# A spectral filter at its own row pitch, one Newton chain on VectorE, and 14 output buffers for the last generator

## The chip, the cores and the metric

The kernel runs on one core of a Trainium2 chip. A core has TensorE (PE: matmuls into PSUM, with the load of weights, PEld, beside them), VectorE (DVE), ScalarE (ACT), GpSimd (POOL) and SyncE (SP), which issues all the DMAs of this kernel. The metric is the device time of one launch in microseconds (us); lower is better. The time before the change is 369.65 us, the median of five runs between 368.98 and 370.34.

## The reference, cut to what matters

A block with two residual halves, its output and the gradients of all its inputs but one:

```python
def _A_ref(x, w_r, w_i):                       # spectral mixer
    X = rfft2(x, axes=(-2, -1))                # x: (1, 2048, 448)
    X = X * (w_r + 1j * w_i)                   # w: (2048, 225)
    return irfft2(X, s=(S, D), axes=(-2, -1))

def _B_ref(x, w1, b1, w2, b2):                 # token MLP, F = 1792
    h = _layernorm(x)
    u = gelu(einsum("bsd,sf->bdf", h, w1) + b1)
    return transpose(einsum("bdf,fs->bds", u, w2) + b2, (0, 2, 1))

h  = x + _A_ref(_layernorm(x), w_r, w_i)
h2 = h + _B_ref(_layernorm(h), w1, b1, w2, b2)
# outputs: h2 and vjp(grad_out) for x, w_r, w_i, w1, b1, w2, b2
```

Everything that goes in and comes out is bfloat16. The filter W has S = 2048 rows (one for each frequency along the sequence) of DF = 225 columns (half of 448, plus 1). Its gradient has the same shape and is output 2 (real part) and 3 (imaginary part).

## The kernel before, in words

The 2-D Fourier transforms are done as matmuls with cosine and sine tables that the kernel makes itself. A transform along D works on rows (`row_a`, `row_b`), one along the sequence is split in two steps, the second of which (`s2_stage`) works on 16 groups g of frequencies, 128 on the partitions, with (group, real or imaginary part, column) in the free dimension. Columns are padded there from 225 to KW = 226.

PE's order is written out by hand. Beside the chain of the transforms runs a list `pending` of generators that hold independent matmuls, and `fill(n)` takes n pieces from it wherever the transforms would leave PE without work. In the forward pass that list is `dg_gen` (the gradient at the GELU's output, 14 blocks of 16 matmuls, each with weights that come by a transposing DMA from w2, `load_w2T`); in the backward pass it is `gw_gen`, once for the gradient of w2 (output 6) and once for that of w1 (output 4).

The stages on PE in order of time are: rows of x with dG blocks (to about 50 us), the forward `s2_stage` with multiplication by W (50 to 86), the inverse rows (86 to 104), the MLP forward and its output (105 to 199), the MLP backward (199 to 246), the backward `s2_stage` (about 263 to 304), the inverse rows for the gradient of x with the second `gw_gen` (about 310 to 353), and the rest of that generator (to 361).

What the change and the prediction touch, by the lines of the kernel before:

- Row statistics and 1/sigma of the first layer norm. `ln_stats` runs on DVE. Rows 0 to 3 take a square root on ACT; rows 4 and 5 take a Newton chain on GpSimd (`newton_gp`, lines 367 to 376: 10 small operations on 128 x 2 values), called at line 844; rows 6 to 15 take the same chain two by two (line 879). `scale_R(t)` on DVE needs 1/sigma of row t; its result rX is the moving operand of `row_a(t)` on PE, whose stationary operand is made by `fold_prep` on DVE. `newton` (lines 353 to 365) is the same chain with 9 operations for DVE; before the change nothing calls it.
- The load of W. `w_load` (line 567) brings each plane (real, imaginary) of W into a helper region rB with four DMAs: partitions 0 to 63, 64 to 111, 112 to 127 and one row apart. Rows for partitions from 64 up have to be in reverse order of the groups, so they are loaded in forward order, one long run for a partition, and `w_place` (line 576) copies all of W from rB to its place `W_view_F` in rG, with the groups of the upper half reversed: 16 copies of 64 x 4 x 225, each given to ACT or DVE by `evac`, which weighs the two engines' loads (`Meter`). The copies are spread over the forward `s2_stage`, two by two from c2 = 3 on (line 672). The first four DMAs are issued in rows 9 to 12, the other four when the forward `s2_stage` begins, in SP's order T W W W W T T T, where T is a weight transpose for dG (line 897).
- The multiplication. `w_mult` (line 697) makes two products of a pair of groups with the real and the imaginary plane, broadcast over the two parts (128 x 904 elements), and two sums, all on DVE. In the backward pass `bwd_mult` (line 1189) does the same with the conjugate, and makes the gradient of W from two more products and two sums, written over W in place.
- W between the passes. It is stored to DRAM (`w_d`, line 915) and loaded again into rC (line 1250). Its gradient goes out from rC with `w_io` (line 551): eight DMAs, whose SBUF side is runs of 225 elements, spread over the rows of the last stage (`GW_AT`).
- Output buffers. Both `gw_gen` generators evict PSUM into the ring `ost`, six buffers of 1024 columns in rO (line 1200). An eviction into a buffer waits until the store from it, six buffers ago, has landed. rG holds `goT`, the moving operand of the first generator, which is done before the second one starts.

Of the kernel before, what the change touches and what calls it, by code (L numbers as in the profile page):

```python
# [98 lines left out]
class Ring:  # L99
# [20 lines left out]
def kernel(  # L120
# [58 lines left out]
    def evac(out, in_, scale=None):  # L179
        n = int(np.prod(in_.shape[1:]))  # L180
        if load[0] + sc.cost('copy', n, False) <= load[1] + ve.cost('tensor_copy', n, in_.dtype == BF16):
            if scale is None:
                sc.copy(out=out, in_=in_)
            else:
                sc.activation(out=out, in_=in_, func=ACT.Copy, scale=scale)
        elif scale is None:
            ve.tensor_copy(out=out, in_=in_)
        else:
            ve.tensor_scalar(out=out, in0=in_, scalar1=scale, scalar2=None, op0=ALU.mult)
# [89 lines left out]
    smc = mem.tile([P, 2, 16], BF16, name="smc")  # L279

    h_d = dram.tile([S, D], BF16, name="h_d")
    w_d = dram.tile([P, NG * 2 * KW], BF16, name="w_d")


    x_pt = A_x[0].rearrange("(p t) d -> p t d", t=NT)
# [259 lines left out]

    W_view_F = cut(rG, 0, NG, 2, KW)
    W_view_B = cut(rC, 0, NG, 2, KW)

    def w_io(Wv, dr, di, store):
        for c_, d in ((0, dr), (1, di)):
            for p0, p1, g0, g1, row, dims in ((0, 64, 0, 16, 0, [[16 * DF, 4], [1, 16 * DF]]),
                                              (64, 112, 0, 16, 112, [[-DF, 48], [1, DF]]),
                                              (112, 128, 1, 16, 127, [[-DF, 15], [1, DF]]),
                                              (112, 128, 0, 1, 64, [[1, DF]])):
                sb = Wv[p0:p1, g0:g1, c_, 0:DF]
                d_ap = bass.AP(d.tensor, d.offset + row * DF, [[P * DF, 16]] + dims)
                if store:
                    nc.sync.dma_start(out=d_ap, in_=sb)  # L560
                else:
                    nc.sync.dma_start(out=sb, in_=d_ap)
                yield

    W_rows = cut(rB, 0, 2, NG, DF)

    def w_load():
        for c_, d in ((0, A_w_r), (1, A_w_i)):
            for p0, p1, j0, j1, row, dims in ((0, 64, 0, 16, 0, [[16 * DF, 4]]), (64, 112, 0, 16, 97, [[-16 * DF, 3]]),
                                              (112, 128, 0, 15, 113, []), (112, 128, 15, 16, 64, [])):  # L570
                nc.sync.dma_start(out=W_rows[p0:p1, c_, j0:j1, :],
                                  in_=bass.AP(d.tensor, d.offset + row * DF,
                                              [[P * DF, 16]] + dims + [[1, (j1 - j0) * DF]]))
                yield

    def w_place():
        for g in range(0, NG, 4):
            for c_ in range(2):
                for p0, p1, src in ((0, 64, W_rows[0:64, c_, g:g + 4, :]),
                                    (64, P, W_rows[64:P, c_, NG - 1 - g:(NG - 5 - g if g < 12 else None):-1, :])):  # L580
                    evac(out=W_view_F[p0:p1, g:g + 4, c_, 0:DF], in_=src)
                    yield

    r452_ring = ring(r452, 0, 8, 2, KW)
    Xs = cut(rX, 0, NG, 2, KW)
# [72 lines left out]
    def s2_stage(get_x, on_mult, ml, n_fill, gap, make_inv, after_fwd=None, scale=None):  # L658
        flush()
        nh = NG // 2  # L660
        xs, ys = {}, {}

        lag = 2 + ml
        for c2 in range(nh + lag):
            if c2 < nh:
                xs[c2] = get_x(c2)
                if make_inv and c2 < 4:
                    gen_inv_s(4 + c2)
                    if c2 in (1, 2):
                        gen_inv_d(c2 - 1)  # L670
            for i in range(2):
                if make_inv and c2 >= 3:
                    next(wp, None)
                    next(wp, None)
                if c2 < nh:
                    g = 2 * c2 + i
                    px = ps_ff()
                    pv = px[:, 0:452].rearrange("p (c k) -> p c k", c=2)
                    mm(pv, lhsT=Vt[:, g, :], rhs=D2[:, g, :, :], start=True, stop=False)
                    mm(pv[:, 0, :], lhsT=Ut[:, g, :], rhs=D2[:, g, 1, :], start=False, stop=False)  # L680
                    mm(pv[:, 1, :], lhsT=Un[g], rhs=D2[:, g, 0, :], start=False, stop=True)
# [14 lines left out]

    def w_mult(c2, xc, Wv, conj):
        y = Y_ring.next()
        wr = Wv[:, 2 * c2:2 * c2 + 2, 0:1, :].broadcast_to([P, 2, 2, KW])
        wi = Wv[:, 2 * c2:2 * c2 + 2, 1:2, :].broadcast_to([P, 2, 2, KW])  # L700
        p1, p2 = p_ring.next(), p_ring.next()
        ve.tensor_tensor(out=p1, in0=xc, in1=wr, op=ALU.mult)
        ve.tensor_tensor(out=p2, in0=xc, in1=wi, op=ALU.mult)
        ve.tensor_tensor(out=y[:, :, 1, :], in0=p1[:, :, 0, :], in1=p2[:, :, 1, :],
                         op=(ALU.add if conj else ALU.subtract))
        ve.tensor_tensor(out=y[:, :, 0, :], in0=p1[:, :, 1, :], in1=p2[:, :, 0, :],
                         op=(ALU.subtract if conj else ALU.add))
        return y
# [90 lines left out]
    def rstd_of(a, b):  # L799
        return newton(mvx[:, a:b, 1], rstd_x[:, a:b], slice(a, b))  # L800
# [31 lines left out]
    nc.vector.memset(csF[:, 0, :, 0:1], 0.0)  # L832
    Rs.update({t: scale_R(t) for t in range(2, 4)})
    ve.tensor_scalar(out=ident[:], in0=krow[:, 0:P], scalar1=pcol, scalar2=None, op0=ALU.is_equal)
    gp_.memset(W_view_F[:, :, :, DF:KW], 0.0)
    w_loads = w_load()
    uv = gen_UV()
    gen_inv_cols(0)
    gen_inv_cols(1)
# [1 line left out]
    fold_prep(xn, 1)  # L841
    for t in (4, 5):
        ln_stats(xn, t, mvx)
    newton_gp(mvx[:, 4:6, 1], rstd_x[:, 4:6], slice(4, 6))
    fill(6)
    turn_biases = load_biases()
    Meter.side, Meter.every, Meter.count = [], 1, 0
# [40 lines left out]
        fill(FILL_B[t])  # L888
    for i in range(2):
        gen_neg(UTn[:, 8 * i:8 * i + 8, :], UTt[:, 8 * i:8 * i + 8, :])  # L890
    wp = w_place()
    gp_.memset(csF[:, 0, :, 0:1], 1.0)
    fill(20)

# [17 lines left out]
    s2_stage(fwd_x, fwd_mult, ML_F, 3, 24, True)  # L912
    drain()

    nc.sync.dma_start(out=w_d[:], in_=rG[:, 0:NG * 2 * KW])

    w1c_ring = Ring([cut(r, o, NT, 256) for r, o in ((r2, 0), (r2, NT * 256), (rO, S))])

# [270 lines left out]
    def bwd_mult(c2, xc):  # L1189
        xs = Xs[:, 2 * c2:2 * c2 + 2, :, :]  # L1190
        y = w_mult(c2, xc, W_view_B, True)
        p1, p2 = p_ring.next(), p_ring.next()
        gw = W_view_B[:, 2 * c2:2 * c2 + 2, :, :]
        ve.tensor_tensor(out=p1, in0=xc, in1=xs[:, :, 0:1, :].broadcast_to([P, 2, 2, KW]), op=ALU.mult)
        ve.tensor_tensor(out=p2, in0=xc, in1=xs[:, :, 1:2, :].broadcast_to([P, 2, 2, KW]), op=ALU.mult)
        ve.tensor_tensor(out=gw[:, :, 0, :], in0=p1[:, :, 0, :], in1=p2[:, :, 1, :], op=ALU.add)
        ve.tensor_tensor(out=gw[:, :, 1, :], in0=p1[:, :, 1, :], in1=p2[:, :, 0, :], op=ALU.subtract)
        return y

    ost = ring(rO, 0, 6, S // 2)  # L1200
    o4 = out_4.rearrange("(p t) f -> p t f", t=NT)

    def gw_gen(n, rhs, width, store):
        for u in range(n // 2):
            st = ahead.pop(0)

# [17 lines left out]
            for c in range(0, 4, 2):  # L1224
# [14 lines left out]
                for i in range(2):  # L1239
                    for k in range(3):  # L1240
                        whole(pv, w, c + 1, i, k, False, k == 2)
                        if k == 2:
# [1 line left out]
                        yield  # L1244

    pending.append(gw_gen(NFB, lambda c, k, a, b: goT[a:b, k, c * 512:(c + 1) * 512], S,
                          lambda j, a, n, o: nc.sync.dma_start(out=out_6[j * P:(j + 1) * P, a:a + n], in_=o[:, 0:n])))
    pending.append(gw_gen(NT, lambda c, k, a, b: du_t[a:b, 4 * c:min(NFB, 4 * c + 4), k, :], F,
                          lambda t, a, n, o: nc.sync.dma_start(out=o4[:, t, a:a + n], in_=o[:, 0:n])))
    nc.sync.dma_start(out=rC[:, 0:NG * 2 * KW], in_=w_d[:])  # L1250
    for t in range(NT - LAG, NT + 2):
        if t == NT - 2:
            fill(8)
# [77 lines left out]
```

## Time and profile before

| What | Value |
|---|---|
| median of 5 runs | 369.65 us (368.98 to 370.34) |
| profiled execution, its own time | 369.65 us |
| its span in the trace | 367.9 us |
| granted TensorE clock, mean | 0.994 |
| PE busy | 345.1 us, 94% |
| DVE, ACT, GpSimd busy | 255.9, 203.5, 73.0 us |
| first matmul, last matmul ends | 7.99 us, 361.22 us |
| DMA | 81.63 MB, 148250 packets; its main queue busy 91.5% of 16 engines' span |
| copies of W into place (`w_place`) | 9 on DVE, 387 ns each; 7 on ACT, 946 ns each |
| products with W | 16 forward at 624 ns, 16 backward at 621 ns |

A span is the time from the first to the last event of the trace; the run's time holds what lies around it as well. Times within the trace count from the span's start. In the busy table, PE 345.1 (94%) x2121 means that 2121 matmuls cover 345.1 us. A group's line names the source line (most operations carry line 79 or 215, those of the helpers that issue them), the engine, the operation, output <- inputs with shapes and the count, then busy time, mean ns of one, and the idle time before them with what ended it. In the table of 40 slices, each digit is the busy share of 9.2 us in tenths.

### The profile page before, as it was taken

To read this page: it belongs to the slowest core of one execution; us is meant where nothing else is said; L and a number is where in the kernel's file an instruction comes from. 1 tells how busy PE (TensorE), PEld (TensorE's weight loads), DVE (VectorE), ACT (ScalarE), POOL (GpSimd) and SP (SyncE) were. 2 spreads that over 40 slices of the span, in tenths; PEclk is the share of its full clock that TensorE was granted. 3 is DMA by queue.
4 is the path that set the end of the run, shared out by engine and by line. 5 is a ranking of instruction groups with operands and counts; after the bars stand their busy time and mean duration, and the time that the engine had idled before them with its cause. 6 is when DMAs were issued, how large, how long until landed. Compare 5 with 4: busy or idle time off the path is not lost.

```text
span 367.9 us, 6394 instructions
## 1 busy us (share of the span) xinstructions
PE 345.1 (94%) x2121; PEld 184.9 (50%) x2121; DVE 255.9 (70%) x641; ACT 203.5 (55%) x426; POOL 73.0 (20%) x240
## 2 busy tenths in 40 slices
PE   1888999899999999999999999999999999999992
PEld 0455765455645555555555656653444543545441
DVE  7698839963957888683247666673887873788881
ACT  3748738856966545323313455554567664676751
POOL 8867000000220000010002222200000000566640
PEclk9999999999999999999999999999999999999997
DMA  8999999749999999998959687479768899998997
GB/s 211 305 216 212 178 199 182 146 135 300 290 304 344 324 294 238 220 273 184 201 133 192 155 168 157 102 229 325 205 198 232 231 198 247 230 213 268 198 203 236
DMA packets 148250, 81.63 MB, mean 222 GB/s; under 512 B 95545, under 2 KB 140601, under 8 KB 147833
## 3 DMA queue, kind: packets, MB, share of 16 engines
q1 hardware_dynamic: 148216, 81.23, 91.5%
q8 instruction: 16, 0.26, 0.3%
q14 instruction: 18, 0.14, 0.1%
HBM read 27.56 MB, written 23.89 MB: 140 GB/s over the span
## 4 chain that ended last, share of the span: by engine, by line
PE 77%; ACT 5%; DMA 5%; POOL 5%; DVE 4%; issue 2%; POOLq 0%; DVEq 0%; ACTq 0%
PE ps_mm L215 62%; PE ps_ff L215 15%; DMA out_dram<-rO 3%; DMA rO<-in_B_w_dram 2%; ACT rO L79 2%; ACT rG L79 1%; DVE r L79 1%; ACT Ut L79 1%; DVE stats L79 1%; DVE rO L79 1%; DVE rA L79 1%; POOL cols L394 1%; POOL cols L395 1%; ACT rX L79 0%; POOL cols L444 0%
## 5 line engine op out<-in xcount | busy, mean ns | idle before, releaser
L215 PEld LDWEIGHTS <-r 128*128 128x128 bf16 (+1 forms) x628 | 60.3, 105 | 49.3 <-issue 1.9
L215 PEld LDWEIGHTS <-rS 128*128 128x128 bf16 (+2 forms) x528 | 44.3, 98 | 49.6 <-DVE rS L79 9.5
L79 ACT CAST rO<-ps_mm 128x512 bf16<-128x512 f32 (+1 forms) x75 | 40.2, 567 | 26.1 <-PE ps_mm L215 19.7
L1130 POOL TENSOR_SCALAR lcol<-lcol 128x1 f32<-128x1 f32 x32 | 18.9, 591 | 149.3 <-ACT r L79 149.1
L215 PE MATMUL ps_mm<-rD,r 128*128 128x448 bf16 x224 | 44.5, 352 | 0.0
L79 DVE CAST rO<-ps_mm 128x512 bf16<-128x512 f32 (+1 forms) x45 | 28.4, 644 | 20.8 <-PE ps_mm L215 15.3
L215 PEld LDWEIGHTS <-rst 128*128 128x128 bf16 (+1 forms) x320 | 24.0, 97 | 29.0 <-issue 13.2
L215 PE MATMUL ps_mm<-rC,rE 128*128 128x448 bf16 x144 | 35.4, 364 | 0.9 <-DMA rE<-in_B_w_dram 0.5
L215 PE MATMUL ps_mm<-rG,rst 128*128 128x512 bf16 (+1 forms) x160 | 35.0, 380 | 0.0
L79 ACT CAST r<-ps_ff 128x452 bf16<-128x452 f32 x54 | 28.9, 537 | 10.0 <-PE ps_ff L215 9.6
L215 PE MATMUL ps_mm<-rB,r 128*128 128x448 bf16 x160 | 31.2, 352 | 0.1
L215 PE MATMUL ps_mm<-r,rst 128*128 128x512 bf16 (+3 forms) x160 | 31.2, 353 | 0.0
L79 ACT ACTIVATE r<-ps_mm,rstd_h 128x448 bf16<-128x448 f32 x16 | 10.1, 633 | 29.3 <-PE ps_mm L215 29.3
L215 PE MATMUL ps_ff<-csI,rAT 113*128 113x448 bf16 x108 | 24.9, 353 | 0.6 <-ACT rAT L79 0.4
L79 DVE SCALAR_TENSOR_TENSOR r<-ps_mm,b2col,r 128x448 bf16<-128x448 f32 x16 | 10.9, 682 | 19.9 <-PE ps_mm L215 18.4
L79 ACT ACTIVATE r<-rC 128x448 bf16<-128x448 bf16 x16 | 9.1, 571 | 26.7 <-DMA out_dram<-r 21.8
L79 ACT ACTIVATE rG<-rG 128x896 bf16<-128x896 bf16 x14 | 13.3, 950 | 14.9 <-DVE rG L79 14.7
L215 PE MATMUL ps_mm<-rE,rS 128*128 128x448 bf16 x112 | 21.5, 352 | 0.0
L215 PEld LDWEIGHTS <-rO 128*128 128x128 bf16 (+1 forms) x165 | 15.6, 98 | 11.2 <-DMA rO<-in_B_w_dram 0.9
L79 ACT CAST rS<-ps_ff 128x512 bf16<-128x512 f32 x30 | 17.7, 589 | 4.3 <-PE ps_ff L215 4.3
L215 PE MATMUL ps_mm<-rC,rO 128*128 128x448 bf16 x80 | 19.1, 352 | 0.5 <-DMA rO<-in_B_w_dram 0.5
L215 PE MATMUL ps_ff<-csF,rS 112*128 112x226 bf16 x128 | 17.7, 260 | 1.7 <-ACT rS L79 1.7
(173 smaller groups left out, 599.8 us busy)
## 6 DMA issues: line engine op xcount, KB each, us to landing
out_dram<-rO SPq DMA_DIRECT2D x44, 256.0 KB
r<-in_B_w_dram SPq DMA_DIRECT2D x5, 1024.0 KB
r<-r SPq DMA_DIRECT2D x16, 226.0 KB
r<-r SPq DMA_DIRECT2D x32, 113.0 KB
rS<-in_B_w_dram SPq DMA_DIRECT2D x4, 896.0 KB
out_dram<-r SPq DMA_DIRECT2D x32, 112.0 KB
out_dram<-rO SPq DMA_DIRECT2D x16, 192.0 KB
rO<-in_B_w_dram SPq DMA_DIRECT2D x2, 1024.0 KB
```

What stands on the lines that cost most here:

```text
L79: fn(**kw)
L215: nc.tensor.matmul(out, lhsT=lhsT, rhs=rhs, start=start, stop=stop)
L394: gp_.tensor_scalar(out=gtmp, in0=in0, scalar1=scalar, scalar2=None, op0=ALU.mult)
L395: gp_.tensor_tensor(out=out, in0=gtmp, in1=in1, op=ALU.add)
L1130: gp_.tensor_scalar(out=m1, in0=ms, scalar1=-1.0 / D, scalar2=None, op0=ALU.mult)
```

## The change

W keeps its own row pitch of 225 and is laid out by part, group, column, both in rG (forward) and in rC (backward). It is loaded by `w_io` straight to its place, with the reversal of the groups done by the DMA's DRAM side, one run of 225 elements for each row of the upper partitions; `w_load`, `w_place` and the pad's memset go. `w_mult` multiplies 225 columns and leaves the pad column of the products unwritten; what comes of it stays in pad columns and reaches no output. The gradient of W is written at the same pitch, and stored with one long run for each of partitions 0 to 63. The chain of rows 4 and 5 is `newton` on DVE in place of `newton_gp`. The second `gw_gen` gets a ring of eight buffers in rG and the six in rO.

```diff
-    w_d = dram.tile([P, NG * 2 * KW], BF16, name="w_d")
+    w_d = dram.tile([P, NG * 2 * DF], BF16, name="w_d")
...
-    W_view_F = cut(rG, 0, NG, 2, KW)
-    W_view_B = cut(rC, 0, NG, 2, KW)
+    W_view_F = cut(rG, 0, 2, NG, DF)
+    W_view_B = cut(rC, 0, 2, NG, DF)
...
-                sb = Wv[p0:p1, g0:g1, c_, 0:DF]
+                sb = Wv[p0:p1, c_, g0:g1, :]
...
-    def w_load():
...
-    def w_place():
...
-                if make_inv and c2 >= 3:
-                    next(wp, None)
-                    next(wp, None)
...
-        wr = Wv[:, 2 * c2:2 * c2 + 2, 0:1, :].broadcast_to([P, 2, 2, KW])
-        wi = Wv[:, 2 * c2:2 * c2 + 2, 1:2, :].broadcast_to([P, 2, 2, KW])
+        wv = Wv.rearrange("p c g k -> p g c k")[:, 2 * c2:2 * c2 + 2]
+        wr = wv[:, :, 0:1, :].broadcast_to([P, 2, 2, DF])
+        wi = wv[:, :, 1:2, :].broadcast_to([P, 2, 2, DF])
         p1, p2 = p_ring.next(), p_ring.next()
-        ve.tensor_tensor(out=p1, in0=xc, in1=wr, op=ALU.mult)
-        ve.tensor_tensor(out=p2, in0=xc, in1=wi, op=ALU.mult)
+        ve.tensor_tensor(out=p1[:, :, :, 0:DF], in0=xc[:, :, :, 0:DF], in1=wr, op=ALU.mult)
+        ve.tensor_tensor(out=p2[:, :, :, 0:DF], in0=xc[:, :, :, 0:DF], in1=wi, op=ALU.mult)
...
-    gp_.memset(W_view_F[:, :, :, DF:KW], 0.0)
-    w_loads = w_load()
+    w_loads = w_io(W_view_F, A_w_r, A_w_i, False)
...
-    newton_gp(mvx[:, 4:6, 1], rstd_x[:, 4:6], slice(4, 6))
+    for fn in rstd_of(4, 6):
+        fn()
...
-    nc.sync.dma_start(out=w_d[:], in_=rG[:, 0:NG * 2 * KW])
+    nc.sync.dma_start(out=w_d[:], in_=rG[:, 0:NG * 2 * DF])
...
-        gw = W_view_B[:, 2 * c2:2 * c2 + 2, :, :]
+        gw = W_view_B.rearrange("p c g k -> p g c k")[:, 2 * c2:2 * c2 + 2]
...
-        ve.tensor_tensor(out=gw[:, :, 0, :], in0=p1[:, :, 0, :], in1=p2[:, :, 1, :], op=ALU.add)
-        ve.tensor_tensor(out=gw[:, :, 1, :], in0=p1[:, :, 1, :], in1=p2[:, :, 0, :], op=ALU.subtract)
+        ve.tensor_tensor(out=gw[:, :, 0, :], in0=p1[:, :, 0, 0:DF], in1=p2[:, :, 1, 0:DF], op=ALU.add)
+        ve.tensor_tensor(out=gw[:, :, 1, :], in0=p1[:, :, 1, 0:DF], in1=p2[:, :, 0, 0:DF], op=ALU.subtract)
...
-    def gw_gen(n, rhs, width, store):
+    def gw_gen(n, rhs, width, store, ost):
...
-                          lambda t, a, n, o: nc.sync.dma_start(out=o4[:, t, a:a + n], in_=o[:, 0:n])))
-    nc.sync.dma_start(out=rC[:, 0:NG * 2 * KW], in_=w_d[:])
+                          lambda t, a, n, o: nc.sync.dma_start(out=o4[:, t, a:a + n], in_=o[:, 0:n]),
+                          Ring(ring(rG, 0, 8, S // 2).views + ost.views)))
+    nc.sync.dma_start(out=rC[:, 0:NG * 2 * DF], in_=w_d[:])
```

Instruction for instruction, the order on PE is the same before and after. DVE has 9 more small operations early and 9 fewer copies in the forward `s2_stage`; ACT has 7 fewer copies; in a few places an eviction goes to the other of the two engines. SP issues as many DMAs as before, in the same places.

More of the change, by code (lines that the diff above doesn't have):

```diff
@@ L563, in w_io @@
                 yield
-    W_rows = cut(rB, 0, 2, NG, DF)
-    def w_load():
[L568 to L574, printed above, removed]
-    def w_place():
[L577 to L582, printed above, removed]
     r452_ring = ring(r452, 0, 8, 2, KW)
@@ L890 @@
         gen_neg(UTn[:, 8 * i:8 * i + 8, :], UTt[:, 8 * i:8 * i + 8, :])
-    wp = w_place()
     gp_.memset(csF[:, 0, :, 0:1], 1.0)
@@ L1246 @@
     pending.append(gw_gen(NFB, lambda c, k, a, b: goT[a:b, k, c * 512:(c + 1) * 512], S,
-                          lambda j, a, n, o: nc.sync.dma_start(out=out_6[j * P:(j + 1) * P, a:a + n], in_=o[:, 0:n])))
+                          lambda j, a, n, o: nc.sync.dma_start(out=out_6[j * P:(j + 1) * P, a:a + n], in_=o[:, 0:n]), ost))
     pending.append(gw_gen(NT, lambda c, k, a, b: du_t[a:b, 4 * c:min(NFB, 4 * c + 4), k, :], F,
-                          lambda t, a, n, o: nc.sync.dma_start(out=o4[:, t, a:a + n], in_=o[:, 0:n])))
-    nc.sync.dma_start(out=rC[:, 0:NG * 2 * KW], in_=w_d[:])
+                          lambda t, a, n, o: nc.sync.dma_start(out=o4[:, t, a:a + n], in_=o[:, 0:n]),
+                          Ring(ring(rG, 0, 8, S // 2).views + ost.views)))
+    nc.sync.dma_start(out=rC[:, 0:NG * 2 * DF], in_=w_d[:])
     for t in range(NT - LAG, NT + 2):
```

## The prediction

> **What bounds the kernel now.** I read the busy table and the 40 slices first, then the waits of TensorE (PE), then the timeline around each wait, then windows of 4 us.
>
> ```profile
> PE 345.1 (94%) x2121; PEld 184.9 (50%) x2121; DVE 255.9 (70%) x641; ACT 203.5 (55%) x426; POOL 73.0 (20%) x240
> PE   1888999899999999999999999999999999999992
> PE ps_ff L215 <- DVE rX L79: 8.5, 2, 8.0
> PE ps_ff L215 <- ACT rS L79: 1.7, 1, 1.7
> PE ps_ff L215 <- DVE rS L79: 1.5, 1, 1.5
> PE ps_ff L215 <- ACT rX L79: 1.2, 2, 0.9
> PE ps_mm L215 <- DMA rO<-in_B_w_dram: 0.5, 1, 0.5
> ```
>
> PE is the bound: the span is 367.9 us and PE is idle for 22.8. The change leaves PE's order as it is, matmul for matmul. So the time can move only by PE's gaps: about 8.0 us before its first matmul, a few us of waits up to 105 us (the lines above are waits of PE, in total, times, longest), and the tail, since PE ends at 361.22 (1.22 us busy in the window that starts at 360). Between 105 and 353 us nearly every window shows PE full. All the change does in those 250 us costs nothing as long as PE stays full there.
>
> These are the places of the gaps that the change touches:
>
> ```profile
> 18.77 0.25 DVE L79 TENSOR_SCALAR rX<-Rm,rstd_x 128x128 bf16<-128x128 bf16 x1 [2.92 <-POOL rstd_x L376]
> 19.38 0.65 PE L215 MATMUL ps_ff<-rX,rS 128*128 128x128 bf16 x4 [1.49 <-DVE rS L79]
> 51.87 4.67 SPq L294 DMA_TRANSPOSE rO<-in_B_w_dram  x1
> 59.31 0.55 PE L215 MATMUL ps_mm<-rC,rO 128*128 128x448 bf16 x2 [0.53 <-DMA rO<-in_B_w_dram]
> 61.79 4.82 ACT L79 COPY rG<-rB 64x900 bf16<-64x900 bf16 x5
> 67.23 0.35 PE L215 MATMUL ps_ff<-r,Vt 128*128 128x452 bf16 x1 [0.89 <-ACT rX L79]
> 361.65 0.86 ACT L79 CAST rO<-ps_mm 128x512 bf16<-128x512 f32 x2 [2.25 <-DMA out_dram<-rO]
> 362.76 1.02 DVE L79 CAST rO<-ps_mm 128x512 bf16<-128x512 f32 x2 [3.95 <-DMA out_dram<-rO]
> 364.09 0.81 SPq L1249 DMA_DIRECT2D out_dram<-rO  x2
> ```
>
> Each line is start, length, engine, what, and in brackets the idle time and its releaser. The reader sees VectorE (DVE) waiting for GpSimd's Newton chain, ScalarE (ACT) blocked by placing copies, and the last evictions waiting for output buffers after PE has finished.
>
> **The change, part by part.**
>
> *Newton chain of rows 4 and 5.* DVE is idle from 15.84 (end of the statistics of rows 6 and 7) to 18.77. The change puts nine [128 x 2] operations on DVE before those statistics. The nearest rows are the aggregate at 0.15 us (two in 0.30) and a 128x1 scale at 0.149; 9 x 0.15 = 1.35. So rX starts at 15.84 + 1.35 = 17.2, 1.5 us earlier. From 20 to 32 us DVE is full (3.97, 4.00, 4.00 of 4) and the chain of waits runs over it into ACT and to PE at 30.2, so the whole stretch moves by that amount. Bounds: the cheapest small DVE row, a 128x2 memset at 0.06, gives 2.92 - 0.54 = 2.4; a 128x16 scalar_tensor_tensor at 0.23 gives 2.92 - 2.07 = 0.85, and 0.5 if the x quarter of rows 8 to 11 (issued at 13.43) is what DVE meets next. I take 1.5, the kind of row nearest in size. What is late next: the chain of rows 6 and 7 stays on GpSimd, starts about 1.4 later (16.24 to 17.6) but alone. Its 10 steps at 0.27 (15.42, 15.69, 15.96 in the trace) end near 20.3; its first reader, the scale of row 6, moves from 23.16 to 21.7, so 1.4 us of cover remain. The dG blocks that PE interleaves keep their weights in time: the transpose issued at 14.06 takes the queue until 17.19 and is first used near 22.9.
>
> *Placing copies.* Nine go from DVE (387 ns each, 3.5 us) and seven from ACT (946 ns, 6.6 us), with one 0.24 us memset on GpSimd. In the trace five on ACT (61.79 to 66.61) hold back the eviction of ps_ff that PE needs: 0.89 us at 67.23 and 0.33 at 68.10. Both gaps go: 1.2 us. The rest was hidden under PE. Bounds 0.5 (another eviction waits in its place) to 1.5 (with the 0.3 of issue around them).
>
> *W loaded in place.* Partitions 64 to 127 now arrive row by row, in runs of 225 elements, 450 bytes; before, every partition came as one run of up to 7,200 bytes. Per plane that is 48 x 16 + 16 x 15 + 16 = 1,024 small packets, 64 on each of 16 DMA engines. No load of this kind is in the trace; the nearest is the store of gradients of W (L560), which goes in 450 byte runs:
>
> ```profile
> 332.00:336.00 4.00, 4.00 (x27) 1.90 (x26) 2.76 (x8) 2.79 (x7) 2.03 (x6) 1.00 1.12 340
> 340.00:344.00 4.00, 4.00 (x28) 1.87 (x27) 3.00 (x8) 3.26 (x8) 2.53 (x7) 1.00 1.05 117
> 352.00:356.00 4.00, 4.00 (x26) 1.90 (x24) 3.80 (x11) 2.29 (x7) 3.12 (x8) 1.00 0.97 189
> ```
>
> The last two columns are the share of the DMA engines and GB/s. With large runs, 340/16/1.12 = 19.0 GB/s per busy engine; with such stores in flight (issued at 350.20 and 354.17), 189/16/0.97 = 12.2. 450 bytes take 24 ns by the one and 37 by the other: 13 ns x 64 = 0.85 us more per plane. Bounds: 0 (no cost per run), and 2.6 us by the worst window, 340 to 344 with a transpose in it (7.0 GB/s, 64 ns). The first plane is cheap: the DMA share falls to 0.33 between 47 and 48 us, so the backlog clears. The second, issued at 49.42, stands on SP's queue just ahead of the weight transpose at 51.87 for which PE already waits 0.53 at 59.31. So PE's wait grows by 0.9. The three transposes after it have 3 us and more: the next is first used at 64.65. The first multiply by W runs at 61.5, some 10 us after the last W load is issued, and its old cover, the copies, is not needed.
>
> *Row pitch of 225 in the multiplies.* W, and in the backward pass the gradient of W, now start on odd elements in every other row: 32 multiplies of 904 become 900, and 16 sums write at odd starts. I cost this at nothing, because of these rows:
>
> ```profile
> L79 DVE TENSOR_TENSOR rS<-rX,rG 128x904 bf16<-128x904 bf16 x16 | 9.3, 624 | 0.4
> L79 DVE TENSOR_TENSOR rS<-rA 128x448 bf16<-128x448 bf16 x32 | 11.0, 385 | 0.6
> L79 DVE TENSOR_TENSOR r<-r 128x448 bf16<-128x448 bf16 x32 | 12.6, 395 | 1.1
> L79 DVE COPY rG<-rB 64x900 bf16<-64x900 bf16 x9 | 3.5, 387 | 0.1
> ```
>
> rS<-rA is the fold: one operand runs backwards from element 447, an odd start, and takes 385 ns against 395 for a dense pair. The copy reads rows of 225, forwards or in reverse row order, at 379 to 397 ns for 900, as fast as the 0.389 us of a dense 128x896 scale. So neither odd starts nor odd rows slow the nearest instructions. [...]
>
> *Stores.* Half of each gradient plane now goes out in 7,200 byte runs: the same 0.85 us of DMA time per plane comes back, near 324 and 350 us, where PE is full. I count it only as less backlog at the end.
>
> *Output buffers.* The second weight-gradient generator gets 14 buffers in place of 6. Its evictions stop waiting for stores. PE ends at 361.22; then one 256 wide eviction (0.4) and 0.31 from eviction to issue (363.78 to 364.09) put the last stores at 361.9 instead of 364.09: 2.2 us. The DMA engines are nearly full there (1.07 and 0.99 from 356 to 364), so some of it is backlog that cannot end sooner: I take 2.0. Bounds: 0 (all backlog) to 2.8 (with the lighter stores).
>
> **Sum.** -1.5 - 1.2 + 0.9 - 2.0 = -3.8 us. The profiled execution took 369.65 us, of which 367.9 are the span, and it is also the median of the five runs (368.98 to 370.34). So 369.65 - 3.8 = 365.85, about 365.9. Its own range, with not all terms at their bounds at once: 364.0 to 368.4.
>
> **Rivals.**
> 1. *The tail is bound by DMA.* Buffers let the stores queue up sooner but the queue ends when it did. For it: the full shares above. Against it: only 0.41 in the last 4 us, and issue at 364.09 follows evictions. Then -1.8: 367.8.
> 2. *The loads in place are slow.* 2.6 us on each plane, with the backlog of the first not cleared, give +5.2 at 59.31 in place of 0.9: 370.2, no change that can be told. Against it: DMA is a third busy at 47 us.
> [...]
> 4. *The change doesn't reach PE at the start.* If DMA or an x load holds the stretch from 20 to 30 us, the 1.5 goes: 367.4.
>
> **Chances.** Forecast 0.64, first rival 0.11, second 0.09, third 0.09, fourth 0.07. A measurement of this kernel tells 0.2%, 0.74 us, from no change. The forecast and rivals 1 and 4 are faster (0.82, less 0.02 for their edges); rival 2 splits 0.06 same, 0.03 slower. With the edges: faster 0.80, same 0.08, slower 0.12. The range has to leave out rival 3 and little else: 363.9 to 370.2.
>
> **What would show it.** Right: no wait of DVE for rstd_x near 18 us and PE's 1.49 us gone; PE not waiting for ACT rX near 67; PE's wait for rO near 59 between 1 and 2 us; multiplies of 128x900 near 0.62; no eviction waiting for out_dram after PE's end, and less than 5 us from there to the end of the span. Wrong: multiplies above 0.7, a wait of PE of over 3 us for weights between 55 and 75, or a tail that still lasts 6.7 us.

## The result, and the profile after

| | before | after |
|---|---|---|
| median of the runs | 369.14 us (367.74 to 371.86) | 370.84 us (368.72 to 374.04) |
| ratio, 95% interval | 1 | 1.0047 (1.0036 to 1.0058) |
| profiled execution, its span | 369.65, 367.9 us | 370.78, 369.0 us |
| last matmul ends, rest of the span | 361.22, 6.7 us | 364.38, 4.6 us |

The change made the kernel slower by 1.7 us; 365.9 was forecast. The ratios of this document leave out executions over 1.5% above the fastest of their kernel, of which there were 1 of 11 in e14 and 5 of 11 in e15, and none elsewhere. The first view is PE's waits in the changed kernel (us in total, times, longest; the first of them is the wait before the first matmul):

```profile
PE ps_ff L215 <- DVE rX L79: 7.0, 1, 7.0
PE ps_ff L215 <- DMA r<-r: 3.2, 1, 3.2
PE ps_mm L215 <- DMA rO<-in_B_w_dram: 2.8, 1, 2.8
PE ps_ff L215 <- ACT rS L79: 1.7, 1, 1.7
PE ps_mm L215 <- DMA rC<-in_grad_out_dram: 0.9, 2, 0.6
PE ps_mm L215 <- DVE rO L79: 0.6, 1, 0.6
```

DVE's rS (1.5) and ACT's rX (1.2) are gone from the list, as the first two terms of the sum said. Two waits for DMA have taken their place. The first is new: r from r, a reshape from SBUF to SBUF that the forward transform needs. The second is the weight transpose, whose wait was 0.5 and was to become 1.4. The chain of waits of the changed kernel shows what each one followed (start, length, what):

```profile
43.58 0.98 ACT r L79 x2
...
44.58 7.00 DMA r<-r
...
53.99 9.03 DMA rO<-in_B_w_dram
```

The transpose went out at 53.99 instead of 51.87 and took 9.03 us to land where it had taken 7.39. SP's queue explains the late start:

```profile
45.20 6.18 SPq L294 DMA_TRANSPOSE rO<-in_B_w_dram  x1
51.44 2.46 SPq L562 DMA_DIRECT2D rG<-in_A_w_i_dram  x4
53.99 6.22 SPq L294 DMA_TRANSPOSE rO<-in_B_w_dram  x1
```

The transpose at 45.20 kept SP for 6.18 us; the same one had kept it for 2.25. Not all of that is the short runs: with long runs and PE as early (e1 and e16 below) it is 4.04, and the rest of the difference is not explained. The windows of 1 us show what the DMA engines did meanwhile. Their columns are length, busy time and count of PE, PEld, DVE, ACT and POOL, then the granted clock, the DMA share and GB/s:

```profile
42.00:43.00 1.00, 1.00 (x8) 0.50 (x6) 1.00 (x3) 0.58 (x1) 0.00 (x0) 1.00 1.24 96
57.00:58.00 1.00, 1.00 (x8) 0.63 (x7) 0.61 (x3) 0.75 (x4) 0.00 (x0) 1.00 1.31 95
62.00:63.00 1.00, 0.00 (x0) 0.00 (x0) 0.00 (x0) 0.00 (x0) 0.00 (x0) 1.00 0.90 179
64.00:65.00 1.00, 1.00 (x5) 0.45 (x3) 0.72 (x2) 0.00 (x0) 0.00 (x0) 0.50 0.84 188
65.00:66.00 1.00, 1.00 (x5) 0.55 (x4) 0.98 (x2) 0.00 (x0) 0.00 (x0) 0.50 1.64 72
67.00:68.00 1.00, 1.00 (x8) 0.61 (x7) 0.97 (x3) 0.37 (x1) 0.00 (x0) 0.98 1.08 243
```

At 42 and at 57 us the DMA engines are more than full (1.24, 1.31) and move only 96 and 95 GB/s. These are the stretches in which the lower half of each plane of W comes in. The view of DMA packets gives the rate for stretches that hold nothing else, first the changed kernel from 41 to 43 us (504 runs of 450 bytes), then the kernel before from 38 to 40 us (64 runs of 7,200 bytes and 15 packets of 4 bytes):

```profile
DMA packets 504, 0.23 MB, mean 113 GB/s; under 512 B 504, under 2 KB 504, under 8 KB 504
q1 hardware_dynamic: 504, 0.23, 125.7%
DMA packets 79, 0.46 MB, mean 230 GB/s; under 512 B 15, under 2 KB 15, under 8 KB 79
q1 hardware_dynamic: 79, 0.46, 110.5%
```

The lower half of a plane is 64 partitions x 16 rows x 450 bytes = 460,800 bytes: 4.1 us at 113 GB/s, 2.0 us at 230. After the second wait the granted clock is 0.50 from 64 to 67 us: five matmuls a microsecond where there are eight.

The rest of the two traces: a block of 16 dG matmuls starts at 86.45 in place of 82.98 (+3.5), some of it is won back over the full stretch (the same four matmuls at 354.68 in place of 352.51, +2.2), PE's end is +3.2, and the span's end +1.1.

Two terms are to be seen in the changed kernel's groups of instructions of DVE:

```profile
L79 DVE TENSOR_TENSOR rS<-rX,rG 128x900 bf16<-128x900 bf16 x16 | 9.4, 629 | 0.6
L79 DVE TENSOR_TENSOR rS<-rS,rC 128x900 bf16<-128x900 bf16 x16 | 9.3, 625 | 0.1
L79 DVE TENSOR_TENSOR rC<-rS 128x450 bf16<-128x450 bf16 x16 | 5.6, 391 | 0.3
```

The products with W take 629 and 625 ns (624 and 621 before), the gradient's sums 391 (390 before): the row pitch costs nothing. And this is the Newton chain in DVE's timeline, first and last of nine operations, then the scale that had waited:

```profile
13.60 0.24 DVE L79 TENSOR_SCALAR mvx<-mvx 128x2 f32<-128x2 f32 x1
...
15.25 0.16 DVE L79 SCALAR_TENSOR_TENSOR rstd_x<-nt_f,rstd_x 128x2 f32<-128x2 f32 x1
...
16.61 0.22 DVE L79 TENSOR_SCALAR rX<-Rm,rstd_x 128x128 bf16<-128x128 bf16 x1
```

It lasts 1.8 us and rX starts at 16.61 in place of 18.77, without a wait. Last, the tail in the timeline (PE, then SP's queue):

```profile
360.12 4.26 PE L215 MATMUL ps_mm<-r,rS 64*128 64x512 bf16 x23 [0.64 <-DVE rO L79]
...
363.80 0.79 SPq L560 DMA_DIRECT2D out_dram<-rC  x1
365.04 0.81 SPq L1227 DMA_DIRECT2D out_dram<-rG  x2
```

No eviction waits for the store of a buffer any more, but PE itself waits here for an eviction, which it did not before: with the loads of DVE and ACT changed, the planner gives one to DVE behind its last layer-norm row. From 354.68 PE needs 9.7 us to its end; before it was 8.7.

### The profile page after: what moved, and what is told of

It reads as the page before. It is cut to its first block, busy times and chain, and to the rows that moved or that the text cites. A ratio compares the mean times of both kernels' runs of the same rounds, so it can differ in the third digit from the quotient of the medians.

```text
span 369.0 us, 6345 instructions
## 1 busy us (share of the span) xinstructions
PE 346.9 (94%) x2121; PEld 186.5 (51%) x2121; DVE 252.4 (68%) x639; ACT 198.6 (54%) x421; POOL 71.5 (19%) x229
## 4 chain that ended last, share of the span: by engine, by line
PE 81%; DMA 5%; DVE 4%; ACT 4%; POOL 2%; issue 2%; POOLq 0%; DVEq 0%; ACTq 0%
PE ps_mm L215 65%; PE ps_ff L215 16%; DMA rO<-in_B_w_dram 2%; DMA r<-r 2%; ACT rO L79 2%; DVE stats L79 1%; DMA rA<-in_A_x_dram 1%; ACT Ut L79 1%; DVE r L79 1%; DVE rA L79 1%; ACT r L79 0%; POOL nt_f L375 0%; DVE rS L79 0%; DVE mvx L79 0%; ACT rAT L79 0%
## 5 line engine op out<-in xcount | busy, mean ns | idle before, releaser
L1108 POOL TENSOR_SCALAR lcol<-lcol 128x1 f32<-128x1 f32 x32 | 19.8, 617 | 148.2 <-ACT r L79 148.2
L215 PE MATMUL ps_mm<-rC,rE 128*128 128x448 bf16 x144 | 36.8, 375 | 1.4 <-DMA rC<-in_grad_out_dram 0.9
L79 ACT CAST rO<-ps_mm 128x512 bf16<-128x512 f32 (+1 forms) x50 | 27.5, 581 | 14.4 <-PE ps_mm L215 12.4
L79 DVE CAST rO<-ps_mm 128x512 bf16<-128x512 f32 (+1 forms) x30 | 19.5, 659 | 11.8 <-PE ps_mm L215 11.8
L215 PE MATMUL ps_mm<-rC,rO 128*128 128x448 bf16 x80 | 20.2, 369 | 2.8 <-DMA rO<-in_B_w_dram 2.8
L79 ACT ACTIVATE rG<-rG 128x896 bf16<-128x896 bf16 x14 | 13.3, 950 | 14.9 <-DVE rG L79 14.7
L215 PEld LDWEIGHTS <-rE 128*128 128x128 bf16 x148 | 14.4, 102 | 10.1 <-issue 3.3
```

Of the source, the lines that this page charges most:

```text
L79: fn(**kw)
L215: nc.tensor.matmul(out, lhsT=lhsT, rhs=rhs, start=start, stop=stop)
L1108: gp_.tensor_scalar(out=m1, in0=ms, scalar1=-1.0 / D, scalar2=None, op0=ALU.mult)
```

## The experiments

Every ratio is to the kernel before, run on the same chip beside the experiment.

| Run | Ratio, 95% interval |
|---|---|
| e1 changed kernel, load undone | 0.9945 (0.9925 to 0.9965) |
| e2 W's part alone | 1.0064 (1.0042 to 1.0086) |
| e3 Newton part alone | 0.9978 (0.9960 to 0.9996) |
| e4 output buffers alone | 0.9992 (0.9978 to 1.0005) |
| e5 long runs in place, rows not reversed | 0.9906 (0.9876 to 0.9936) |
| e6, e9 runs at 512 byte pitch, lower half left out | 1.0150, 1.0158 |
| e7, e10 runs of 900 bytes, lower half left out | 1.0096, 1.0134 |
| e8, e16 long runs, placed by GpSimd | 0.9906 (0.9868 to 0.9943), 0.9934 (0.9899 to 0.9969) |
| e11 as e8, six output buffers | 0.9921 (0.9893 to 0.9948) |
| e12 as e8, stores of W's gradient earlier | 0.9966 (0.9939 to 0.9993) |
| e13 as e8, 450 byte runs | 1.0043 (1.0017 to 1.0069) |
| e14 as e8, 900 byte runs | 0.9956 (0.9927 to 0.9984) |
| e15 changed kernel, second plane issued later | 1.0011 (0.9971 to 1.0050) |

**One part at a time (e1 to e4).** e1 is the changed kernel with W loaded into rB in long runs and placed by the 16 copies of before, at the new pitch:

```diff
-    w_loads = w_io(W_view_F, A_w_r, A_w_i, False)
+    w_loads = w_load()
...
+                    evac(out=W_view_F[p0:p1, c_, g:g + 4, :], in_=src)
```

> The changed kernel with the load of W as before: long runs into rB, 16 copies on ACT and DVE (pitch 225, Newton on DVE and 14 buffers stay). Theory (the 450 byte runs of the load delay what stands behind them on SP's queue): PE's waits of 3.2 us for the reshaped rows near 50 us and of 2.8 us for weights near 63 us go back to 0 and 0.5, the 1.2 us behind the copies come back, the 1.9 us gained at the start and about 2 us of the end stay: 365.0 to 366.5. Rival (PE, 1.9 us earlier, only runs into transfers that were late all along): both waits stay within 1 us of the changed kernel's, 369 to 370.5.

Measured 0.9945, against 1.0047 for the changed kernel: loading in place costs 0.0102 x 369.14 = 3.8 us (some 0.9 either way), with what the copies saved already taken off. The median is 367.0, so all the rest of the change gains 2.0 us, less than expected. Both waits are down to about 1 us (1.2 for rO, 1.0 for r, where 0.5 and 0 were expected), and ACT's rX is back with 1.0.

e2 takes the changed kernel with `newton_gp` and the six buffers of before:

```diff
-    for fn in rstd_of(4, 6):
-        fn()
+    newton_gp(mvx[:, 4:6, 1], rstd_x[:, 4:6], slice(4, 6))
...
-                          Ring(ring(rG, 0, 8, S // 2).views + ost.views)))
+                          ost))
```

> The filter part of the change alone: pitch 225, W loaded in place, no copies; Newton chain of rows 4 and 5 on GpSimd and 6 buffers as before. Theory: 3 us of wait for the reshaped rows, 2 more for weights, 1.5 from a lower clock after them, less 1.2 of the copies: 373 to 375. Rival (late transfers met by an earlier PE): 368 to 369.5, since PE is not earlier here.

The median is 371.33, between the two. The waits of e2 show why:

```profile
PE ps_mm L215 <- DMA rO<-in_B_w_dram: 2.6, 1, 2.6
PE ps_ff L215 <- DMA r<-r: 1.0, 1, 1.0
```

The reshape r lands at 51.5 to 51.6 us in both kernels, but PE comes to it at 50.71 in e2 and at 48.51 in the changed kernel. So the wait of 3.2 us for r is in good part time that had been gained at the start: with the short runs, PE comes earlier only to wait there. And in e2's profile no half clock follows the wait for rO.

e3 and e4 put those two parts alone into the kernel before:

```diff
-    newton_gp(mvx[:, 4:6, 1], rstd_x[:, 4:6], slice(4, 6))
+    for fn in rstd_of(4, 6):
+        fn()
```

> The kernel before with the Newton chain of rows 4 and 5 on DVE, nothing else. Theory: PE is 1.5 to 1.9 us earlier from 30 us to the end: 367.2 to 367.8. Rival (an earlier PE meets late transfers): no change, 368.8 to 369.4, with a new wait of PE for a DMA before 65 us.

```diff
-    def gw_gen(n, rhs, width, store):
+    def gw_gen(n, rhs, width, store, ost):
...
+                          Ring(ring(rG, 0, 8, S // 2).views + ost.views)))
```

> The kernel before with 14 output buffers for the second weight-gradient generator, nothing else. Theory: the end of the span follows PE's end by 4.6 us in place of 6.7: 366.8 to 367.8, or 1 us more if PE waits for an eviction near the end as it does for 0.6 us in the changed kernel. Rival (the end is bound by the DMA queue): 368.8 to 369.4.

In us of 369.14: W's part +2.4, Newton -0.8, buffers -0.3 (-0.8 to +0.2), together +1.3, near the +1.7 of the whole. So the loss is all in W's part. e3 (368.31) falls between its theory and its rival, e4 (368.82) in the range of its rival.

**What of the load is slow (e5, e6, e7).** e5 keeps the loads in place and their number of instructions, but a partition of the lower half comes as one run, its rows in forward order; the reversal is left out.

```diff
+        for p0, p1, g0, g1, row, dims in ((0, 64, 0, 16, 0, [[16 * DF, 4]]), (64, 112, 0, 16, 97, [[-16 * DF, 3]]),
...
+            nc.sync.dma_start(out=W_view_F[p0:p1, c_, g0:g1, :], in_=bass.AP(d.tensor, d.offset + row * DF,
+                              [[P * DF, 16]] + dims + [[1, (g1 - g0) * DF]]))
```

> The changed kernel, with W still loaded straight into its place, but the 16 rows of a partition of the lower half of the planes (partitions 64 to 127) come as one run of 7,200 bytes instead of 16 runs of 450. The rows of these partitions stay in the order of the input, so the reversal is left out and the outputs behind W are not the reference's; instructions and their number are unchanged. Theory (the number of small runs is the price, about 98 ns each on a DMA engine in the trace of the changed kernel): both waits of PE shrink, 3.2 to about 1.0 for the reshaped block (r from r) and 2.8 to 1.2 or less for the transposed weights; against the run with the load undone (367.0) it also has no copies, and that run still had 1.0 us of waits for ACT: 366.0, at most 367.0. Rival (what costs is the load in place as such: the direct loads land in rG and so depend on something that the loads into rB did not, or their place on the queue): waits stay above 2 us each, 370 to 371.

0.9906, waits of 0.7 for r and 1.3 for rO: loading straight into rG costs nothing that shows once the runs are long. The rival that blames the place or the dependence falls.

e6 and e7 send the small runs to a scratch area, at a pitch of 512 bytes and in pairs of 900 bytes; W's lower half is set to 0 by a memset. e9 and e10 are the same with the memset moved.

```diff
+    W_s = cut(rB, 0, 2, NG, 256)
...
+    gp_.memset(W_view_F[64:P], 0.0)
```

> The changed kernel with the same 450 byte runs for the lower half of W, the same number and order, but each landing in a scratch area at a pitch of 512 bytes, so that each run starts on a multiple of 512 bytes in its partition; W's lower half itself is left out (set to 0 by one GpSimd memset). Theory (each run costs, wherever it lands): waits of PE of 2 to 3 us for r and for rO stay, 370 to 371.5. Rival (the odd landing address, 450 bytes apart, is what makes a run slow): DMA windows at 41 to 44 and 56 to 61 us go back to above 200 GB/s, the two waits shrink to about 1 us each, 366 to 367.5.

> The changed kernel with the lower half of W loaded into a scratch area in runs of 900 bytes, two rows each, so half as many runs with the same bytes (the 15th row of partitions 112 to 127 is left out, and W's lower half itself is left out, set to 0). Theory (price per run, 98 ns): half the extra DMA time, some 3 us less per plane; the waits of PE fall to about 1.5 to 2 us for r and 1 to 2 us for rO, 367.5 to 369. Rival (price per byte of such a transfer, or a fixed price of the instruction): waits as in the changed kernel, 370 to 371.5. [...]

> As the run with runs on multiples of 512 bytes, but the memset of W's left-out lower half moved from the start, where it delayed PE's first matmul from 7.0 to 12.1 us, to 44 us, where GpSimd is idle. Theory (every 450 byte run costs, wherever it lands): PE waits 2 to 3 us each for r and for rO, ratio to the kernel before 1.002 to 1.008 (the changed kernel: 1.0047). Rival (the odd landing address is the price): waits near 1 us each, ratio 0.989 to 0.994, as with long runs (0.9906).

> As the run with 900 byte runs of two rows, with the memset moved in the same way. From the low-rate stretches of the two earlier traces, 5.1 us for 64 runs of 450 bytes an engine (80 ns a run) and 3.3 us for 32 of 900 (103 ns a run): a fixed 57 ns and 0.051 ns a byte. Theory (fixed price per run): about 1.9 us less DMA time per plane than with 450 bytes; PE waits 1.2 to 2.2 us for r and 0.3 to 1.8 for rO, ratio 0.992 to 0.998. [...] Second rival (price per byte): 1.002 to 1.008.

Their times say nothing about the loads. GpSimd's schedule put the memset at the start in all four, as the timeline of e9 shows:

```profile
3.58 6.13 POOL L882 MEMSET rG<- 64x7200 bf16 x1
```

It held back what DVE needs for the first rX, and PE began at 12.1 to 13.2 us instead of 7.0. Only their DMA rates can be read, 84 to 93 GB/s in e6 from 60 to 63 us: no better at a pitch of 512 bytes. The question was asked again with e13 and e14.

**The version that follows, and number against address (e8, e13, e14, e16).** GpSimd is idle from 36 to 84 us. In e8 W's upper half is loaded in place in long runs, the lower half in long runs into rB, and GpSimd places it, reversed, in eight copies of 64x900. e16 is the same kernel again, on the chip of e13 and e14.

```diff
+                dst = W_view_F if p0 == 0 else W_rows
...
+    def w_place(c_):
+        for g in range(0, NG, 4):
+            gp_.tensor_copy(out=W_view_F[64:P, c_, g:g + 4, :],
+                            in_=W_rows[64:P, c_, NG - 1 - g:(NG - 5 - g if g < 12 else None):-1, :])
```

> The version that the theory recommends: W's upper half (partitions 0 to 63) loaded in place in long runs, the lower half in long runs into rB and placed from there, reversed, by eight copies of 64x900 on GpSimd, which is idle from 36 to 84 us; all else as in the changed kernel. The output is the reference's. Theory: waits of PE for r and rO about 1.0 each, no wait for ACT rX (1.0 in the run with the load undone, whose 16 copies sat on DVE and ACT): 366.0, 365.3 to 366.8, faster than both kernels. Rival (the copies on GpSimd slow down what VectorE does beside them, or come too late for the first multiply at 61.5 us): PE waits of 1 us or more for DVE between 60 and 75 us, 367.5 to 369.

> The version with the placing on GpSimd once more, as the ground for the two runs beside it: ratio 0.989 to 0.994 (0.9906 in its first measurement).

Faster than both kernels, by 2.4 to 3.5 us than before. The timeline of e16 shows the copies, 0.9 us each. The last ends at 60.9, and the first two products, from 60.53 on, take 1.39 us beside it where the next two take 1.17:

```profile
45.88 3.59 POOL L579 COPY rG<-rB 64x900 bf16<-64x900 bf16 x4 [11.47 <-DMA rB<-in_A_w_r_dram]
...
57.32 3.58 POOL L579 COPY rG<-rB 64x900 bf16<-64x900 bf16 x4 [5.08 <-DMA rB<-in_A_w_i_dram]
```

e13 and e14 change in it the runs in which the lower half arrives, 450 bytes each on a multiple of 512 bytes, or 900 bytes in pairs of rows, and with them the order in which the eight copies read them; e14 has one more DMA for each plane.

```diff
-                in_=W_rows[64:P, c_, NG - 1 - g:(NG - 5 - g if g < 12 else None):-1, :])
+                in_=W_s[64:P, c_, g:g + 4, 0:DF])
```

> The version with the placing on GpSimd, but the lower half of W comes into the scratch area in the 450 byte runs of the changed kernel, each starting on a multiple of 512 bytes in its partition, in the order in which it is used; the eight copies on GpSimd remain. The output is the reference's. Only the number of runs and their length differ from the version with long runs. Theory (each run costs some 80 to 98 ns, wherever it lands): PE's waits rise from 0.9 and 1.2 to 2 to 3 us each for r and rO, ratio 1.000 to 1.007. Rival (the odd landing address was the price): 0.989 to 0.993.

> The same with runs of 900 bytes (two rows of W each), so half as many; the GpSimd copies swap the rows of a pair. The output is the reference's. Theory (57 ns a run and 0.051 ns a byte, from the low-rate stretches of earlier traces): waits of PE 1.2 to 2.2 us for r and 0.5 to 1.5 for rO; ratio 0.993 to 0.998. [...]

e13 has the changed kernel's time (1.0043) and its waits:

```profile
PE ps_mm L215 <- DMA rO<-in_B_w_dram: 3.5, 1, 3.5
PE ps_ff L215 <- DMA r<-r: 2.8, 1, 2.8
```

e16 beside it, on the same chip:

```profile
PE ps_ff L215 <- DMA r<-r: 1.0, 1, 1.0
PE ps_mm L215 <- DMA rO<-in_B_w_dram: 0.9, 1, 0.9
```

So the short runs are the price, 0.0109 x 369.14 = 4.0 us (some 1.6 either way), and the odd landing address is none of it. e14 lies between, 0.8 us above e16 (the intervals overlap) and 3.2 below e13. The rate in stretches of the first and of the second plane that hold nothing but these runs, e13 first:

```profile
41.00:42.00 1.00, 1.00 (x11) 0.81 (x10) 0.39 (x1) 0.40 (x2) 0.00 (x0) 1.00 1.26 93
56.00:57.00 1.00, 1.00 (x8) 0.63 (x7) 0.72 (x2) 1.00 (x4) 0.00 (x0) 1.00 1.25 91
```

and e14:

```profile
42.00:43.00 1.00, 1.00 (x10) 0.63 (x9) 0.89 (x3) 0.59 (x1) 0.00 (x0) 1.00 1.19 160
56.00:57.00 1.00, 1.00 (x9) 0.62 (x7) 0.34 (x2) 0.84 (x4) 0.00 (x0) 1.00 1.18 138
```

The traces also have the time of every packet. A 450 byte run takes an engine 69 ns on average in the changed kernel and 73 in e13, a 900 byte run 101 in e14, and a 7,200 byte run 559 in the kernel before, 35 for every 450 bytes. A fixed 45 ns a run and 0.062 ns a byte fit e13 and e14; for 7,200 bytes they give some 490 ns, where 559 were measured. That is an estimate from two points. The profiled execution of e14 took 372.29 us, its median is 368.51, and its clock stands at 0.50 from 52 to 55 us, so of that trace only rates and packet times are used.

**The order on the queue (e15).**

```diff
-            for kind in "TWWWWTTT":
+            for kind in "TTWWWWTT":
```

> The changed kernel with one edit: the four loads of W's second plane are issued one transpose later on SP's queue, behind the transpose of weights that PE waits for (it was issued at 53.99, after them). Theory (the price is paid by what stands behind the small runs in the DMA queue): PE's wait for rO falls from 2.8 to below 1.2 us, the wait for r (from the first plane) stays near 3, and something else is late in place: the first multiply by W at 61.5, or the next transpose (rE, first used at 64.65 before); ratio 0.998 to 1.006. Rival (the wait of 2.8 us has nothing to do with the W loads ahead of it): unchanged wait, 1.0036 to 1.0058.

The wait for rO is gone from the list, so the loads ahead of that transpose did cause it. What stands behind the loads now pays: SP spends 11.77 us on the three rE transposes (7.78 in the changed kernel) and PE waits for rE twice, 1.0 us in all (0.5 in the changed kernel). Another wait, of 2.9 us at 85 to 88 us, has no cause that the trace names; the 12 matmuls behind it take 1.46 us (0.84 in e13). The time is too scattered (367.71 to 375.00, with a median of 372.59 over all 11) to tell a gain from none. That moving the loads is a remedy is not shown.

**The tail (e11, e12).** e11 is e8 with the six buffers of before; e12 is e8 with the gradient's stores issued earlier:

```diff
-                          Ring(ring(rG, 0, 8, S // 2).views + ost.views)))
+                          ost))
...
-    GW_AT = (4, 9, 11, 11, 12, 13, 14, 15)
+    GW_AT = (4, 8, 9, 10, 11, 12, 13, 13)
```

> The version with the placing on GpSimd, with the 6 output buffers of before instead of 14. Theory (the end is set by the stores: in the profile of that version the DMA engines move 352 to 383 GB/s from 360 to 363 us, buffers only let the stores queue sooner): 0.3 us slower than with 14, between 0 and 0.8; ratio 0.991 to 0.993. Rival (my prediction's step: the evictions' wait for buffers is 2.0 us of the path): ratio 0.995 to 0.997, with waits of DVE and ACT of 2 to 4 us for stores from rO after PE's end.

> The version with the placing on GpSimd, with the gradient-of-W stores issued at output rows 4, 8, 9, 10, 11, 12, 13, 13 instead of 4, 9, 11, 11, 12, 13, 14, 15, so that none stands on SP's queue ahead of the last stores of the weight gradient (at 362.46, with the last stores behind it at 362.91, after the last eviction at 362.4). Theory (bytes set the end): within 0.4 us of the version it is made from, ratio 0.989 to 0.992. Rival (SP's queue sets it): the last stores go out up to 0.5 us after the last eviction and the tail after PE falls from 5.3 to some 4.5 us, ratio 0.987 to 0.989. A stronger DMA load on the middle of the tail could also delay the LN rows' stores: then slower.

e11 is as fast as e8 and e16 (0.9921 between 0.9906 and 0.9934). Its timeline, with six buffers:

```profile
358.97 2.02 SPq L1246 DMA_DIRECT2D out_dram<-rO  x4
...
360.95 1.26 DVE L79 CAST rO<-ps_mm 128x512 bf16<-128x512 f32 x2 [0.96 <-PE ps_mm L215]
360.96 0.93 ACT L79 CAST rO<-ps_mm 128x512 bf16<-128x512 f32 x2 [1.72 <-PE ps_mm L215]
...
361.96 0.94 SPq L1246 DMA_DIRECT2D out_dram<-rO  x2
```

The last evictions wait for PE, not for a store, as they do in e2, which also has six. From the start of the last four transform matmuls to the end of the span it is 15.4 us in the kernel before, 14.7 with the buffers alone (e4), 14.7 with W's part alone (e2), 14.3 in the changed kernel and 14.4 in e11. But the same stretch is 15.3 in e3, and 14.1, 14.8 and 15.0 in e1, e16 and e8, all three with the new layout and 14 buffers. Profiles of kernels with the same tail differ by 0.9, so differences of half a us can't be read. What the lines above do show is that W's part, with half of its gradient leaving in long runs and PE's end 1 us later, takes the wait away already; the buffers then add nothing that shows. Which of the two does it was not separated.

e12 was slower than either theory had it: the earlier stores shift the planner's evictions, and its timeline has a new wait of PE:

```profile
356.49 7.75 PE L215 MATMUL ps_mm<-r,rS 128*128 128x512 bf16 x32 [2.81 <-ACT rO L79]
```

## Why the prediction was wrong

- **Newton chain, -1.5.** Right in mechanism, too large: -0.8 (-0.1 to -1.5) by itself. The wait is gone, and in e3, where PE starts as late as in the kernel before, the block of 16 dG matmuls moves from 82.98 to 81.72, 1.3 us. But the nine operations follow each other at 0.20 us, not 0.15, so the chain takes 1.8 us. And a forward transform that comes early can meet the reshape r: PE waits about 1 us for it in e1 and e16, with long runs. The first matmul of the changed kernel's profile starts 1.0 us earlier than before (6.96 in place of 7.99); no term of the sum holds that, and its cause stays open.
- **Placing copies, -1.2.** Right in mechanism: the wait for ACT's rX is gone. Versions with long runs are 0.4 to 1.4 us faster without copies on ACT and DVE (e5, e8, e16 against e1), but the intervals overlap, so the size is not settled.
- **W loaded in place, +0.9.** This step failed. It priced a load in 450 byte runs by a store in such runs, 13 ns more than a long run, "13 ns x 64 = 0.85 us more per plane". Measured, a run takes 69 ns where the same bytes in a long run take 35, so 64 x 34 ns = 2.2 us more per plane. The 37 ns was about right for a store (41 in the packet times of the kernel before), but not for a load. The 24 ns was too low: the window from 332 to 336, which the prediction took for large runs, holds 830 packets of 256 bytes beside longer ones. And "the first plane is cheap" read the wrong moment: the share falls to 0.33 at 47 us, but the reshape that PE needs next is issued at 44.58, inside the first plane's backlog. The trace shows where the time went. The block of 16 dG matmuls starts at 86.45 where e1, with long runs, has 82.47: the wait for r is 2.2 us longer, that for rO 1.6, the half clock after it costs 1.7, and ACT's rX saves 1.0, together 4.5 of which 4.0 are seen. In place of 0.9 the load costs 4.0 to 5.2 us in whole runs (e13 against e16, the changed kernel against e16 and against e5 or e8). The bound of 2.6 us on each plane was near, and the second rival, built on it (370.2), is what happened, with 9 chances in 100. That its number is near is in part luck: it has +0.5, counted from 369.65, where +1.7 from 369.14 came, because its gains at the start and at the end (1.5 and 2.0) were too large, and the clock is not in it.
- **Row pitch, 0.** Held: 629, 625 and 391 ns. No run shows a product or a sum slowed by an odd start, the case that had 0.09 of the chances and that the range was drawn to leave out. But the new layout has fewer odd starts than the prediction read: the two rows of a pair are one run of 450 elements, so the sums write from multiples of 900 bytes, and in the products only the second row of each pair begins on an odd element. So these times say little of odd starts as such; the nearest measure of one stays the fold row of the kernel before, 385 ns from element 447 where a dense pair takes 395.
- **Stores, 0, and output buffers, -2.0.** The first rival was right here in size: the buffers give 0.3 by themselves, and nothing that shows beside the new layout of W; that the DMA engines bind the tail, which is its reason, is not shown. The span does end 4.6 us after PE in place of 6.7, as forecast, but PE ends 1 us later for the eviction that the planner moved; that move was seen in the order of instructions and was given no price. And the 0.31 us from the last eviction to its store did not stay: in e4 the last eviction ends at 361.20, and its store is issued at 362.95, behind a store of W's gradient on SP's queue.
- **Signs.** All signs of being right came but one (PE's wait for rO, 2.8 us in place of 1 to 2), and none of being wrong; the wait above 3 us was for r, where no sign had been set.
- **Sum.** With these sizes, and 4.0 for the load, -0.8 - 1.2 + 4.0 - 0.3 = +1.7; measured +1.7 (1.3 to 2.1). The agreement is closer than the terms are known, the load's 4.0 above all.

## What to carry to other kernels

Price a DMA by the number of contiguous runs on each engine, take the price from a row of the same direction (here 450 bytes took 69 ns in a load and 41 in a store; that the direction makes the difference is not shown), and ask what is issued behind it in the following microseconds; here the loads themselves were never waited for, only what queued after them. If a layout needs short runs, let an idle engine reorder after a long-run load: eight GpSimd copies replaced 2 x 1,024 runs and made the change a gain. A wait that another part of the change takes away already, as the buffers' was, can't be counted a second time, and a gain ahead of a late transfer, as the one at the start was, can be waited away there.

## What the runs showed of the hardware that was not expected

**Short runs.** A 450 byte run from DRAM to SBUF took 69 ns of an engine's time in the changed kernel and 73 in e13, with the queues full (4,096 such runs from SBUF to DRAM in the kernel before took 41 ns each), and landing on 512 byte multiples changes nothing (91 and 93 GB/s in e13, 95 and 96 in the changed kernel). Where the short runs start in DRAM was not varied. Whether it is the direction or the fuller queue that makes a load dearer than a store was not separated. Nor does every short packet cost that much: from 61 to 62 us the changed kernel moves 1,129 packets of 256 bytes, of the transposing weight loads, at 289 GB/s, 18 ns each. Runs of twice the length, 900 bytes, still moved only 138 to 160 GB/s in the windows shown, against 230 for runs of 7,200.

**The clock after a wait.** In windows of 0.1 us the clock of the changed kernel falls to 0.50 at 63.63 us and returns at 67.05, after PE stood idle from 60.23 to 63.07; in e6 it is 0.50 from 67.90 to 71.31 after an idle stretch from 64.1 to 66.7. Each lasts 3.41 us, which costs 1.7 us of PE's work. The idle 3.2 us before 51.7 in the changed kernel had no such sequel, nor had the waits of 2.6 us for rO in e2 and e9: the windows of 1 us after them show a clock of 1.00, to 71 us in e2 and to 70 in e9. So the wait of 2.8 us cost some 4.5, and those of 2.6 in e2 and e9 only their own length. The length of a wait does not tell which kind it is: 2.6 us in e6 is followed by half clock, 3.2 in the changed kernel is not. One difference is to be seen in the changed kernel's trace. Counted back from 63.63 us in stretches of 3.41 us, the last one holds 2.84 us of PE's idle time, while the idle 3.2 us lie across two of them, with 1.74 and 1.47. That this decides it is the author's estimate from this one trace.
